# A linear-attention layer and a gated unit: q in token order, permuted transposes, new loads, stores and work order

## The chip, the cores and the metric

The kernel runs on one core of a Trainium2 chip. Its engines each follow their own instruction queue: PE (TensorE, matmuls), ACT (ScalarE, exponentials and evictions), DVE (VectorE), POOL (GpSimd, which also issues DMAs) and SP (SyncE, which here only issues DMAs). Engines wait for each other by semaphores. The time of a kernel is the device time of one execution in microseconds (us).

## The reference

Eight batches, eight heads, 576 tokens, head size 64, 128 random features; the model width is 512. Inputs and output are float32.

```
def phi(x):
    proj = einsum('bhsd,df->bhsf', x, w_phi)
    proj = proj - max(abs(proj), axis=-1, keepdims=True)
    return concatenate([exp(proj), exp(-proj)], axis=-1)
q_p, k_p = phi(q), phi(k)
kv  = einsum('bhsf,bhsd->bhfd', k_p, v)
z   = sum(k_p, axis=2)
num = einsum('bhsf,bhfd->bhsd', q_p, kv)
den = einsum('bhsf,bhf->bhs', q_p, z)[..., None] + 1e-06
x   = (num / den), heads side by side                # (8, 576, 512)
gate = sigmoid(causal convolution of x over 5 tokens, per channel)
out  = (gate * (x @ w_val)) @ w_out                  # (8, 576, 512)
```

## The kernel before

**Attention of one batch.** k and q of a batch are 4608 rows of 64 numbers each. They lie in SBUF with 128 rows by 36 columns of 64, two columns side by side make 18 blocks of 128 by 128, and the blocks are transposed so that PE can contract over the head size. Five units (four of 4 blocks, one of 2) go through PSUM. For k: `kp` projects a unit (L577), `kmax` (L585, DVE) takes the largest absolute value of each row, `kexp` (L595, ACT) makes exp(proj) and exp(-proj), two instructions of 1024 elements for a full unit. The maxima are not subtracted from k's projections; `ek` (L604, ACT) makes a factor of them, and `vs` (L610, POOL) multiplies v by it, four times per batch. `st` (L620, PE) contracts features with scaled v and a column of the factor, which gives kv and z together, and `kv` evicts it. For q: `qm` projects (L577), `qmax` takes maxima (L585), `mqt` and `mqr` transpose and negate them, `rx` (L682, POOL) spreads them over a block pattern, `qp` (L693 and L698, PE) computes features by tokens and adds the negated maxima with a second matmul, and `qexp` (L706, ACT) makes the two exponentials. Its last, half unit is written with four instructions into a tile of its own, `QTT` (L709). `num` (L719, L726) multiplies by kv and z, and `nrm` (L737, L740, DVE) divides.

**Order of q's tokens.** q is read as one flat array, 36 consecutive rows to a partition, so a unit holds tokens from all over the sequence. Every `num` task of a batch therefore waits for all ten exponentials of q (`allq`), and its output rows are tokens in steps: x comes out in two halves of 144 columns, and tokens 16 and 17 of each run of 18 land in a fifth, half-size piece.

**The gated unit of one batch.** Normalised x is transposed, 128 by 128, by PE (`xtp`, L748, L752) and copied (`xtc`); for batches 6 and 7 (`XB`) two of the three parts go by DMA transposes instead (`xtd`, L755). `halo` (L768, L769, POOL) copies the columns that the convolution needs from the other half. `gate` (L781) is 80 matmuls of 64 by 64 with diagonal weights, `tanh` (L785, ACT) makes the sigmoid, `val` (L791) 32 matmuls, `gv` (L797, DVE) the product, `gvc` (L805, POOL) collects the tokens of the fifth piece of two batches, `out` (L813; L817 for that piece) the output matmuls, `oev` evicts, `odma` (L830, L836) stores rows of 2 KB.

**Loads.** Batch 0's k and q come as float32 from SP's queue and are transposed as float32 (`tp32`, L536). Later batches come as bf16 from POOL's queue, one DMA for k and one for q (L550), batch 1 transposed on PE (L555), batches 2 to 7 by DMA transposes from SP's queue (L565). v comes from SP's queue, batch 1's from POOL's. A copy of one column (`hold`, L509, L512) on POOL keeps a load behind the transpose that frees its buffer.

**The order of the work.** `build` lists tasks with what they wait for. `ORDER` is the list in which they are written out: each engine runs its own tasks in that order, whatever is ready. `FLEX` says which engine takes a task that several could take, `BANKS` which PSUM banks a group of tasks uses. `WARM` and `ZERO` insert dummy matmuls at places of the order; those of `ZERO` add zeros to a finished result (L497, L504).

Of the kernel before, what the change touches and what calls it, by code (L numbers as in the profile page):

```python
# [24 lines left out]
NU = len(UNITS)  # L25
PEB = 1
QPART = ((0, 1), (2, 3, 4))
XB = (6, 7)
HOLDU = 4
NO = 8  # L30
NJ = 2 * NC
XH = R // 2
HALO = 16
XW = HALO + XH
# [4 lines left out]
STD = 1.18  # L39
E1 = D + 1  # L40
QW = 2 * NR

ORDER = (
# [36 lines left out]
)  # L80
FLEX = (
    "AAAAAADAAADDPPPPDDDDAADDDDDDDDDDDDDAAADAAAADDDDAAADDDAADAAADDADAADDDDADDDDADDDDDDAADADDAAAAAA"
)
BANKS = (
    "037362307001454523232323016701676714232367230101676012354423010145454501013660564675601456745010145450101676767014501454"
    "545672012376701230167676745677773567232367232345452301672323232367674545015452343623670101232345454452230145450167676767"
    "010123014501230167450120167364012345236745454555723014545234567232323010123236745230167232346701422010167454567010121656"
    "701456701012301670123010167232367674567023677260123230123230167464644501016701670123676745672345232345450123670157672345"
    "010167452326322345670145670101674545012345012367452345010127452301014545670101765"
)  # L90

# [809 lines left out]
```

## Time and profile before

| what | us |
|---|---|
| runs | 216.2, 217.88, 246.94 (median 217.88) |
| span of the profiled execution, first to last instruction | 215.4 |
| PE busy | 194.6 (90%) |
| ACT busy | 180.6 (84%) |
| DVE busy | 170.2 (79%) |
| POOL busy | 132.9 (62%) |

The profile shows one execution. Its device time outside of the profile is not known; its span is 0.8 us under the fastest of the runs. A row of a group names a line, an engine, an operation, the tile written and the tiles read, a count, the busy time and the mean time of one. A row of the timeline or of the chain begins with its start and its length in us. Matmuls overlap each other: 72 state matmuls of 191 ns each take 1.16 us together, so a chain row divided by its count is the price of one in a row of many.

### The profile page before, as it was taken

To read this page: it belongs to the slowest core of one execution; us is meant where nothing else is said; L and a number is where in the kernel's file an instruction comes from. 1 tells how busy PE (TensorE), PEld (TensorE's weight loads), DVE (VectorE), ACT (ScalarE), POOL (GpSimd) and SP (SyncE) were. 2 spreads that over 40 slices of the span, in tenths; PEclk is the share of its full clock that TensorE was granted. 3 is DMA by queue.
4 is the path that set the end of the run, shared out by engine and by line. 5 is a ranking of instruction groups with operands and counts; after the bars stand their busy time and mean duration, and the time that the engine had idled before them with its cause. 6 is when DMAs were issued, how large, how long until landed. Compare 5 with 4: busy or idle time off the path is not lost.

```text
span 215.4 us, 9005 instructions
## 1 busy us (share of the span) xinstructions
PE 194.6 (90%) x3924; PEld 138.9 (64%) x3944; DVE 170.2 (79%) x257; ACT 180.6 (84%) x267; POOL 132.9 (62%) x172
## 2 busy tenths in 40 slices
PE   2887978778999999989999999999999999899990
PEld 2665566566766767667767677568757766687640
DVE  3299999999699978998899978998699897654510
ACT  3699999999999899998899997999988988634251
POOL 3045999996984649952997099903992879210010
PEclk9999999999999999999999999999999999999998
DMA  6999979999799699979997878979962264864166
GB/s 180 381 226 208 291 162 159 277 198 199 139 165 286 118 153 250 290 130 200 237 279 134 96 165 251 188 151 173 287 211 84 67 161 126 83 168 99 49 188 205
DMA packets 49954, 39.92 MB, mean 185 GB/s; under 512 B 34165, under 2 KB 39541, under 8 KB 49914
## 3 DMA queue, kind: packets, MB, share of 16 engines
q1 hardware_dynamic: 43616, 28.65, 56.8%
q0 software_dynamic: 6032, 10.49, 26.2%
q8 instruction: 31, 0.51, 1.0%
q10 hardware_dynamic: 266, 0.21, 0.3%
q14 instruction: 9, 0.07, 0.1%
HBM read 30.48 MB, written 9.44 MB: 185 GB/s over the span
## 4 chain that ended last, share of the span: by engine, by line
PE 55%; ACT 18%; DVE 15%; issue 4%; DMA 4%; SPq 0%; DVEq 0%; ACTq 0%
PE PS L791 12%; PE PS L781 9%; PE PS L813 9%; ACT QTIL L706 7%; ACT KTIL L595 7%; DVE MQP L585 6%; PE PS L719 5%; PE PS L577 5%; PE PS L620 4%; DVE MK L585 2%; PE PS L693 2%; DMA KTIL<-in_k_dram 2%; DMA XT<-XN 2%; PE PS L536 2%; DVE XN L740 2%
## 5 line engine op out<-in xcount | busy, mean ns | idle before, releaser
L595 ACT ACTIVATE KTIL<-PS 128x1024 bf16<-128x1024 f32 (+1 forms) x80 | 71.8, 965 | 3.5 <-PE PS L577 1.7
L610 POOL TENSOR_TENSOR VT<-VN,EK 128x1152 bf16<-128x1152 f32 x32 | 67.9, 2123 | 2.9 <-ACT EK L604 2.8
L706 ACT ACTIVATE QTIL<-PS 128x1024 bf16<-128x1024 f32 x64 | 62.5, 1051 | 1.9 <-PE PS L698 1.4
L682 POOL TENSOR_TENSOR RX<-MQR,ident 128x512 bf16<-128x512 bf16 (+1 forms) x39 | 36.6, 963 | 36.2 <-DVE MQR L670 32.8
L585 DVE TENSOR_REDUCE MK<-PS 128x8 f32<-128x1024 f32 (+1 forms) x40 | 44.3, 1113 | 2.9 <-PE PS L577 1.2
L585 DVE TENSOR_REDUCE MQP<-PS 128x8 bf16<-128x1024 f32 (+1 forms) x40 | 43.6, 1112 | 2.1 <-PE PS L577 1.2
L791 PE MATMUL PS<-XT,WV 128*128 128x288 bf16 x256 | 34.8, 286 | 0.3 <-DVE GV L797 0.2
L797 DVE SCALAR_TENSOR_TENSOR GV<-TH,PS 128x576 bf16<-128x576 bf16 x32 | 23.8, 752 | 10.4 <-PE PS L791 4.7
L813 PE MATMUL PS<-WOUT,GV 128*128 128x512 bf16 x110 | 29.7, 380 | 1.1 <-issue 0.2
L791 PEld LDWEIGHTS <-WV 128*128 128x128 bf16 x256 | 23.8, 98 | 7.9 <-issue 1.4
L785 ACT ACTIVATE TH<-PS 128x576 bf16<-128x576 f32 x32 | 20.4, 663 | 9.3 <-PE PS L781 5.9
L781 PE MATMUL PS<-XT,GW 64*64 64x288 bf16 x640 | 23.2, 285 | 0.8 <-DMA XT<-XN 0.7
L620 PE MATMUL PS<-VT,KTIL 64*128 64x65 bf16 x1152 | 23.1, 191 | 0.7 <-issue 0.6
L740 DVE TENSOR_TENSOR XN<-PS,RCP 128x512 bf16<-128x512 f32 x32 | 22.1, 692 | 1.4 <-DMA XT<-XN 0.3
L620 PEld LDWEIGHTS <-KTIL 64*128 64x128 bf16 x1152 | 20.7, 95 | 3.3 <-issue 2.3
L719 PEld LDWEIGHTS <-QTIL 128*128 128x128 bf16 x512 | 18.3, 97 | 6.4 <-issue 4.1
L719 PE MATMUL PS<-KV,QTIL 128*128 128x65 bf16 x512 | 20.3, 193 | 0.4 <-DVE MQP L585 0.2
L781 PEld LDWEIGHTS <-GW 64*64 64x64 bf16 x640 | 17.8, 106 | 3.4 <-issue 0.8
L634 ACT ACTIVATE OUTS<-PS 128x512 f32<-128x512 f32 x22 | 13.5, 619 | 7.3 <-PE PS L813 6.1
L813 PEld LDWEIGHTS <-GV 128*128 128x128 bf16 x128 | 11.1, 98 | 11.3 <-issue 0.6
L577 PE MATMUL PS<-W,qT 64*128 64x128 bf16 x288 | 15.2, 219 | 2.7 <-ACT QTIL L706 1.0
L577 PEld LDWEIGHTS <-qT 64*128 64x128 bf16 x288 | 10.7, 95 | 9.1 <-issue 4.3
(79 smaller groups left out, 235.0 us busy)
## 6 DMA issues: line engine op xcount, KB each, us to landing
out_dram<-OUTS SPq DMA_DIRECT2D x32, 256.0 KB, 3.4
VN<-in_v_dram SPq DMA_DIRECT2D x7, 1152.0 KB, 6.4
KQN<-in_q_dram POOLq DMA_DIRECT2D x6, 576.0 KB, 8.3
KQN<-in_k_dram POOLq DMA_DIRECT2D x6, 576.0 KB, 9.6
KTIL<-in_k_dram SPq DMA_DIRECT2D x4, 288.0 KB, 4.3
VN<-in_v_dram POOLq DMA_DIRECT2D x1, 1152.0 KB, 11.5
KTIL<-in_q_dram SPq DMA_DIRECT2D x4, 256.0 KB, 5.0
out_dram<-OUTS SPq DMA_DIRECT2D x14, 64.0 KB, 2.4
```

The source lines that it names most:

```text
L577: nc.tensor.matmul(self.PS[:, t.grp.banks[par], i * P:(i + 1) * P], X[rows, (c0 + i) * P:(c0 + i + 1) * P], self.W2[rows, :], start=True, ...
L585: self.nc.vector.tensor_reduce(o, self.two(t.grp, n * P).rearrange("p a (c f) -> p a c f", f=F), AX.X, ALU.max, apply_absolute_value=True)
L595: self.nc.scalar.activation(self.KTIL[b % 2][:, s, c0:c0 + n, :, :].rearrange("p c a f -> p a c f"), self.two(t.grp, n * P).rearrange("p a ...
L610: nc.gpsimd.tensor_tensor(self.VT[g][:, s, :, 0:D], self.VN[b % 2][:, NC * g:NC * g + NC, :], e.to_broadcast([P, NC, D]), ALU.mult)
L620: nc.tensor.matmul(self.PS[:, t.grp.banks[ab], (s * 2 + x) * E1:(s * 2 + x + 1) * E1], self.KTIL[b % 2][rows, s, J // 2, J % 2, :], self.V ...
L682: self.nc.gpsimd.tensor_tensor(o, *wide(self.MQR[self.mq(b, u)][:, :], self.ident2), ALU.mult)
L706: self.nc.scalar.activation(o, i, AF.Exp, scale=1.0 - 2.0 * s)
L719: nc.tensor.matmul(self.PS[:, t.grp.banks[h // 4], (h % 4) * E1:(h % 4 + 1) * E1], Q[:, s, c % 2, h, (c // 2) * P:(c // 2 + 1) * P], self. ...
L740: nc.vector.tensor_tensor(o.rearrange("p (g h) d -> p g h d", g=ng), n[:, :, :, 0:D], rc.unsqueeze(3).to_broadcast([P, ng, 4, D]), ALU.mult)
L781: self.nc.tensor.matmul(self.PS[o * D:(o + 1) * D, t.grp.banks[par], 0:R], self.GW[r, jj, 4 - m, :], X[r, 4 * a + jj, :, HALO - 8 * s:HALO ...
L791: self.nc.tensor.matmul(self.PS[:, t.grp.banks[par], 0:R], self.WV[:, i, (2 * j + par) * D:(2 * j + par + 2) * D], X[:, 4 * par + i, :, HA ...
L813: nc.tensor.matmul(self.PS[:, t.grp.banks[0], :], GV[:, j, c % 2, (c // 2) * XH:(c // 2) * XH + P], self.WOUT[:, j, c % 2, :], start=(j == ...
```

## The change

The kernel is written anew around another order of q's tokens; the arithmetic is the same.

- q is loaded as bf16 in five pieces of 128 tokens (the last of 64) for all heads, each token run of 8 rows to a partition. A unit then holds consecutive tokens, `num(b, c)` waits only for the two exponentials of unit c and for kv, and `QTIL` holds all tokens in sequence. `QTT`, `GVT`, `halo`, `gvc`, `hold` and the 144-column halves are gone.
- The transposes of x multiply by a permuted identity (`perm`) instead of the identity, which puts the tokens of a transposed block in order. All go through PE; `xtd` is gone.
- Gate, tanh, value and product of batches 0 and 7 are done in two column parts, 0 to 128 and 128 to 288 (`COLS`).
- All of k, q and v, batch 0 too, come from POOL's queue; batch 0 is cast to bf16 by its load and transposed as bf16. SP keeps the DMA transposes and the stores.
- A store writes two consecutive tokens per partition, 4 KB rows; the last one goes in two. The tails of two batches (64 tokens each) share one eviction and two stores.
- `ORDER`, `FLEX` and `BANKS` are new, banks come in pairs (0,1), (2,3), (4,5), (6,7), `ZERO` is gone and `WARM` has two entries. The reciprocal is a task of its own.

```diff
+KLOAD = (((0, 1), (1, 1), (2, 2)), ((0, 4),))
+QLOAD = ((tuple((i, 1) for i in range(5)),) * 2)
+NO = 4
+COLS = {b: ((0, R),) for b in range(B)}
+COLS[0] = ((0, P), (P, R))
+COLS[B - 1] = ((0, P), (P, R))
-    "60:6:1 81:1:1 87:7:2 134:7:1 141:7:1 "
-ZERO = "35:76:7 61:80:5 75:34:1 101:105:1 126:215:8 144:223:1 155:192:4 158:200:1 175:315:6 189:346:1 195:241:2 197:241:2 211:327:1"
+    "11:7:5 54:5:1 "
...
+            for i, (p0, n) in enumerate(KLOAD[b > 0] if w == "k" else QLOAD[b > 0]):
+                x = A("l" + w, b, i, "POOL", fn("load", w, b, p0, n), [G("xd" + w, b - 1)])
...
+                x = A("xp", b, 0, "SP", fn("xpose", w, b), sorted(set(land[w]), key=lambda t: t.idx) + war)
...
+            x = A("lv", b, 0, "POOL", fn("loadv", b), [G("vs", b - 2, g, s) for g in range(2) for s in range(2)])
...
-        allq = [G("qexp", b, u, s) for u in range(NU) for s in range(2)] + [G("kv", b, i) for i in range(2)]
...
-            num = h["num", b, c] = A("num", b, c, "PE", 0.57 if c < 4 else 0.38, fn("num", b, c), allq,
-                                     g, 0 if c < 4 else 2)
+            num = h["num", b, c] = A("num" if c < 4 else "num4", b, c, "PE", fn("num", b, c),
+                                     [h["qexp", b, c, s] for s in range(2)] + [h["kv", b, i] for i in range(2)], g, 0 if c < 4 else 2)
...
-                if i < 2 and b in XB:
-                    xt = h["xtp", b, i] = A("xtp", b, i, "SP", 1.4, fn("xtd", b, i), nrms + war, lat=-0.2)
...
+        for z, (x0, x1) in enumerate(COLS[b]):
+            xs = [h["xtc", b, i] for i in range(3) if i * P < x1 and min(R, (i + 1) * P) > x0 - (1 if x0 else 0)]
+            for j in range(4):
+                g = plan.group("gate", 2)
+                gt = h["gate", b, j, z] = A("gate", b, j, "PE", fn("gate", b, j, x0, x1), xs + h["gw"], g, 3, n=x1 - x0)
...
-        self.QTIL = TT("QTIL", 2, [P, 2, 2, H, 2 * P])
+        self.QTIL = TT("QTIL", 2, [P, 2, H, S])
...
+        for i, n in enumerate((4, 2)):
+            nc.vector.tensor_copy(self.perm[i][:, :].rearrange("p (z x y) -> p z y x", x=8, y=n),
+                                  ident_f[:, :].rearrange("p (z y x) -> p z y x", x=8, y=n))
...
+    def load(self, t, w, b, p0, n):
+        N = self.N[w][b]
+        if w == "k":
+            o = N[:, :, :].rearrange("p y c -> p (y c)").rearrange("p (hp x) -> p hp x", hp=4)[:, p0:p0 + n, :]
+            self.nc.gpsimd.dma_start(o, self.rows("k", b)[:, p0:p0 + n, :])
+            return
+        x = self.src["q"][b]
+        c0 = 4 * p0
+        if p0 < 4:
+            self.nc.gpsimd.dma_start(N[:, c0:c0 + 4, :].rearrange("p y c -> p (y c)"), x[:, p0 * P:(p0 + 1) * P, :].rearrange("h (i t) d -> h i (t d)", i=16))
+        else:
+            self.nc.gpsimd.dma_start(N[:, 16:18, :].rearrange("p y c -> p (y c)"), x[:, 4 * P:S, :].rearrange("h (i t) d -> h i (t d)", i=16))
...
-        if u < 4:
-            o = self.QTIL[b % 2][:, s, :, :, :].rearrange("p a h (k r) -> p a (h k) r", k=2)[:, :, :, u * 32:(u + 1) * 32]
-            self.nc.scalar.activation(o, i, AF.Exp, scale=1.0 - 2.0 * s)
-        else:
-            for a in range(2):
-                self.nc.scalar.activation(self.QTT[:, s, :, a, :].rearrange("p h (k r) -> p h k r", k=2),
-                                          i[:, a, :, :].rearrange("p (h k) r -> p h k r", k=2), AF.Exp, scale=1.0 - 2.0 * s)
+        o = self.QTIL[b % 2][:, s, :, u * P:u * P + n * 32].rearrange("p h (a r) -> p a h r", a=2)
+        self.nc.scalar.activation(o, self.two(t.grp, n * P).rearrange("p a (h r) -> p a h r", h=H), AF.Exp, scale=1.0 - 2.0 * s)
...
-            for y in range(8):
-                nc.tensor.transpose(ps[:, y * P:(y + 1) * P], self.XN[i][:, y // 4, (y % 4) * P:(y % 4 + 1) * P], self.ident[:, :])
+            o = ps.rearrange("p (a j u r) -> p u j a r", a=2, j=4, u=2)
+            for u in range(2):
+                for j in range(4):
+                    nc.tensor.transpose(o[:, u, j], self.XN[i][:, u, j * P:(j + 1) * P], self.perm[0][:, :])
...
+    def out4(self, t, b):
+        for j in range(4):
             for a in range(2):
+                for i in range(2):
                     p0 = a * D + i * 32
+                    self.nc.tensor.matmul(self.PS[p0:p0 + 32, t.grp.banks[0], :], self.GV[(b - 1 + i) % 3][:, j, a, 2 * P:R],
+                                          self.WOUT[:, j, a, :], start=(j == 0), stop=(j == 3))
...
+    def store(self, t, b, kk):
+        d = self.out_d[b][2 * P * kk:2 * P * (kk + 1), :].rearrange("(r a) o -> r (a o)", a=2)
+        self.nc.sync.dma_start(d, self.OUTS[(2 * b + kk) % NO][:, :, :].rearrange("p a o -> p (a o)"))
...
+    def store4(self, t, b, a):
+        eng = self.nc.scalar if t.eng == "ACT" else self.nc.sync
+        d = self.out_d[b - 1:b + 1, 4 * P:S, :].rearrange("i (r a) o -> a i r o", a=2)[a]
+        eng.dma_start(d, self.OUT4[b // 2 % 2][a * D:(a + 1) * D, :])
```

More of the change, by code (lines that the diff above doesn't have):

```diff
@@ L90 @@
 )
 class Task:
-    __slots__ = ("kind", "b", "u", "engs", "durs", "fn", "deps", "grp", "also", "opens", "mode", "eng", "lat", "idx", "wait", "rank")
+    __slots__ = ("kind", "b", "u", "engs", "fn", "deps", "grp", "opens", "mode", "eng", "idx", "n")
 class Group:
     __slots__ = ("kind", "nb", "left", "banks", "idx")
-def out_seq(b, c):
-    return 9 * (b // 2) + (4 * (b % 2) + c)
-LAT = {"PE": 0.17, "ACT": 0.17, "DVE": 0.17, "POOL": 0.2, "SP": 0.7, "DMA": 1.3}
-MSW = 0.05
-def dve(n, ov=0.075):
-    return n / 960.0 + ov
@@ L147, in follow @@
     def follow(self):
-        names = {"A": "ACT", "D": "DVE", "P": "POOL"}
+        names = {"A": "ACT", "D": "DVE", "P": "POOL", "S": "SP"}
         for t, f in zip([t for t in self.tasks if len(t.engs) > 1], FLEX):
@@ L160, in parts, with pieces @@
     return QPART if b == 0 else (tuple(range(NU)),)
+def pieces(b):
+    return ((0, 8), (8, 8), (16, 2)) if b else ((0, 4), (4, 4), (8, 8), (16, 2))
+VE = ("DVE", "ACT")
 def build(plan, em=None):
@@ new lines, in build @@
+            h["idf"] = A("idf", 0, 0, "POOL", fn("c_idf"))
+            h["id"] = A("idb", 0, 0, "DVE", fn("c_idb"), [h["idf"]])
+            h["idc"] = A("idc", 0, 0, "DVE", fn("c_idc"), [h["idf"]])
+            x = A("lw", b, 0, "SP", fn("c_w"))
+            x = A("DMA", b, 0, "DMA", None, [x], n="lw")
+            h["w"] = A("wc", b, 0, "DVE", fn("c_w2"), [x])
+            x = A("lcw", b, 0, "SP", fn("c_cv"))
+            h["lcw"] = A("DMA", b, 0, "DMA", None, [x], n="lcw")
+        land = {"k": [], "q": []}
@@ L256, in build @@
[L256 to L259 removed]
+        if True:
+            x = A("lv", b, 0, "POOL", fn("loadv", b), [G("vs", b - 2, g, s) for g in range(2) for s in range(2)])
+            h["lv", b] = A("DMA", b, 0, "DMA", None, [x], n="lv")
@@ new lines, in build @@
+        if b == 0:
+            x = A("wv", b, 0, "POOL", fn("c_wv"), [])
+            x = A("DMA", b, 0, "DMA", None, [x], n="wv")
+            h["wv"] = A("wvx", b, 0, "POOL", fn("c_wvx"), [x])
+            x = A("wo", b, 0, "POOL", fn("c_wo"), [])
+            h["wo"] = x = A("DMA", b, 0, "DMA", None, [x], n="wv")
+            x = A("wod", b, 0, "SP", fn("c_dupo"), [x])
+            h["wod"] = A("DMA", b, 0, "DMA", None, [x], n="wod")
+            g = plan.group("cw", 1)
+            x = A("cw", b, 0, "PE", fn("c_cw"), [h["lcw"], h["idf"]], g, 0)
+            x = A("cw2", b, 0, "DVE", fn("c_cw2"), [x], g)
+            h["gw"] = [A("cgt", b, i, "POOL", fn("c_gt", i), [x, h["idc"]]) for i in range(2)]
@@ L330, in build @@
-                g = plan.group("xtp", 1)
-                xt = h["xtp", b, i] = A("xtp", b, i, "PE", 0.54 if i < 2 else 0.22, fn("xtp", b, i), nrms, g, 0)
-                h["xtc", b, i] = A("xtc", b, i, ("DVE", "ACT"), (dve(512), act(1024)) if i < 2 else (dve(256), act(256)), fn("xtc", b, i), [xt] + war, g)
-        halo = A("xtc", b, 3, "POOL", 0.6, fn("halo", b), [G("xtc", b, 2)] + [G("gate", b - 2, j) for j in range(4)])
-        xall = [G("xtc", b, i) for i in range(3)] + [halo]
-        for j in range(4):
-            g = plan.group("gate", 2)
-            gt = h["gate", b, j] = A("gate", b, j, "PE", 0.62, fn("gate", b, j), xall, g, 3)
-            h["tanh", b, j] = A("tanh", b, j, "ACT", act(576), fn("tanh", b, j), [gt, G("gv", b - 1, j)], g)
@@ new lines, in gvs @@
+        def gvs(b, x0, x1):
+            return [h["gv", b, j, z] for j in range(4) for z, (y0, y1) in enumerate(COLS[b]) if y0 < x1 and y1 > x0]
+        for kk in range(2):
+            oes = []
+            war = stores[-NO] if len(stores) >= NO else None
+            for a in range(2):
+                g = plan.group("out", 1)
+                o = h["out", b, 2 * kk + a] = A("out", b, a, "PE", fn("out", b, a, kk), gvs(b, kk * P, kk * P + P) + [h["wod" if a else "wo"]], g, 0)
+                oes.append(A("oev", b, a, VE, fn("oev", b, a, 2 * b + kk), [o, war], g))
+                if b == B - 1 and kk == 1:
+                    x = A("st1", b, a, ("SP", "ACT"), fn("store1", b, kk, a), [oes[a]])
+                    x = A("DMA", b, a, "DMA", None, [x], n="st1")
+            if not (b == B - 1 and kk == 1):
+                x = A("st2", b, kk, "SP", fn("store", b, kk), oes)
+                x = A("DMA", b, kk, "DMA", None, [x], n="st2")
+                stores.append(x)
@@ new lines, in build @@
+        if b % 2:
+            g = plan.group("out4", 1)
+            o = A("out4", b, 4, "PE", fn("out4", b), gvs(b, 2 * P, R) + gvs(b - 1, 2 * P, R) + [h["wod"]], g, 4)
+            h["out", b, 4] = h["out", b - 1, 4] = o
+            oe = A("oev", b, 4, VE, fn("oev4", b), [o, G("st4", b // 2 - 2, 0), G("st4", b // 2 - 2, 1)], g)
+            for a in range(2):
+                x = A("st4", b, a, ("SP", "ACT") if b == B - 1 else "SP", fn("store4", b, a), [oe])
+                h["st4", b // 2, a] = A("DMA", b, a, "DMA", None, [x], n="st4")
@@ L365 @@
+    return plan
+EKS = (0,)
+VSD = (0,)
 class Emit:
@@ L859 @@
             warm[int(i)] = (int(bank), int(n))
-        zero = {}
-        for x in ZERO.split():
-            i, k, n = x.split(":")
-            zero[int(i)] = (int(k), int(n))
         for i, t in enumerate(plan.follow()):
-            for _ in range(zero[i][1] if i in zero else 0):
-                em.zero(plan.tasks[zero[i][0]])
             for _ in range(warm[i][1] if i in warm else 0):
```

488 lines of the change are left out of this document (158 added, 330 removed), and 75 rows, old and new, of the table ORDER.

## The prediction

> **What bounds the kernel now.** I read the page's first two parts, then the stretches, then the chain of waits in order of time, and last the groups. The page's shares alone mislead: three engines are over 79% busy, each the limit somewhere else.
>
> ```profile
> span 215.4 us, 9005 instructions
> PE 194.6 (90%) x3924; PEld 138.9 (64%) x3944; DVE 170.2 (79%) x257; ACT 180.6 (84%) x267; POOL 132.9 (62%) x172
> ```
>
> The stretches (start and end, length, then busy time of PE, PEld, DVE, ACT and POOL, granted clock, DMA share, GB/s) separate them:
>
> ```profile
> 5.00:10.00 5.00, 4.29 (x31) 3.36 (x31) 0.45 (x2) 3.08 (x5) 0.00 (x0) 1.00 1.02 370
> 30.00:40.00 10.00, 7.31 (x261) 5.98 (x259) 9.54 (x13) 9.94 (x14) 10.00 (x11) 1.00 1.00 220
> 160.00:170.00 10.00, 9.95 (x232) 7.10 (x232) 8.58 (x11) 9.04 (x15) 5.20 (x6) 1.00 0.22 57
> 200.00:210.00 10.00, 9.95 (x61) 5.60 (x62) 3.69 (x5) 4.16 (x8) 1.05 (x4) 1.00 0.44 128
> ```
>
> At 30 to 40 us ACT is full (9.94 of 10) and PE is not: the attention of the first batches feeds PE too little. At 160 us PE is full and ACT waits now and then. At 200 us PE alone is full: the two last gated units are run off while ACT and DVE are half idle. The timeline and the chain date the turns and give the price of each PE task:
>
> ```profile
> 51.11 1.56 PE L781 MATMUL PS<-XT,GW 64*64 64x288 bf16 x40
> 184.75 1.25 ACT L709 ACTIVATE QTT<-PS 128x256 bf16<-128x256 f32 x4
> ```
> ```profile
> 94.12 0.89 PE PS L748 x16
> 125.28 0.37 PE PS L726 x16
> 133.63 1.16 PE PS L620 x72
> 149.34 0.98 PE PS L719 x32
> 162.27 0.55 PE PS L577 x16
> 180.65 0.21 PE PS L693 x2
> 180.86 0.22 PE PS L698 x2
> 183.74 4.44 DMA XT<-XN
> 195.35 3.19 PE PS L781 x100
> 199.51 3.92 PE PS L791 x32
> 203.43 3.24 PE PS L813 x15
> 209.47 1.00 PE PS L817 x8
> 210.54 0.60 ACT OUTS L634
> ```
>
> The first gate runs at 51.1 us, the last exponential of attention ends at 186.0, PE ends at 210.5, and eviction and store of the last tile take the other 4.9 to 215.4. Per batch these rows give PE: gate 80 at 31.9 ns = 2.55 us; value 32 at 122.5 = 3.92; output 16 at 216 = 3.46 and half a pair of tails 0.50; state 144 at 16.1 = 2.32; numerator 64 at 30.6 = 1.96 and tail 0.37; projections 72 at 34.4 = 2.48; q features 4.5 units at 0.43 = 1.94; transposes of x 18 at 55.6 = 1.00. Sum **20.5 us**, 164.0 for eight batches, 162.2 with the 32 transposes that DMA does here. By the written order, before the first gate PE has done 208 projections (7.15), 8.5 units of q features (3.66), 216 state matmuls (3.48), one numerator (2.33) and one set of transposes (1.0): 17.6. So 144.6 us of PE work take the 159.4 us from 51.1 to 210.5: **a density of 0.907**, in which the 4.44 us wait for the DMA transpose of x lies. From 51 us on the time is PE's work over that density; before it, it is the time to the first gate.
>
> **The change part by part.**
>
> *q in sequence.* Before, each numerator task waits for all ten q exponentials, because a unit holds scattered tokens; after, unit c holds tokens 128c to 128c+127 and its numerator waits for two. With the first batch's gated unit split at column 128, the first gate needs only two normalised units. By the changed order, PE has before it: projections of k and q for two batches (144, 4.95), one batch of q features (1.94), state (2.32), numerator (2.33), transposes (1.0): 12.5 instead of 17.6, and 72 bf16 transposes of the inputs.
>
> When is that? The queue of loads decides. The order issues k0, k1, all of q0, four pieces of q1, two of q2, then v0: 6.2 MB of float32 at the 370 GB/s of the 5 to 10 us row is 16.6 us, and 3 us to a first landing, so v0 is there at about 20.
>
> ```profile
> 8.68 1.94 ACT L595 ACTIVATE KTIL<-PS 128x1024 bf16<-128x1024 f32 x2 [0.39 <-PE PS L577]
> 58.34 2.12 POOL L610 TENSOR_TENSOR VT<-VN,EK 128x1152 bf16<-128x1152 f32 x1
> 60.55 2.12 POOL L610 TENSOR_TENSOR VT<-VN,EK 128x1152 bf16<-128x1152 f32 x1
> 78.10 4.61 POOL L682 TENSOR_TENSOR RX<-MQR,ident 128x512 bf16<-128x512 bf16 x5 [4.39 <-DVE MQR L670]
> 66.11 3.77 ACT L595 ACTIVATE KTIL<-PS 128x1024 bf16<-128x1024 f32 x4
> ```
>
> POOL then does two scalings of v (2.21 each, start to start), three q maxima (2.6 of the 4.61) and one more scaling (the fourth is DVE's): 29 us. State, eviction, numerator, normalising, transposes and copy add 4 to 5. ACT arrives there too: its first exponential is at 8.7 us now, behind float32 transposes, and comes at about 7.5 by my estimate; it has 24 by then, 20 of them at 0.94 and four at half, five copies and two evictions, some 25 us, so 32.5. The first gate comes at **34 us** (31 if loads overlap better, 40 if they land late), 17 us earlier than now.
>
> *PE's total.* 164.0 - 12.5 = 151.5 us are left after the first gate; 151.5 / 0.907 = 167.0. With 34 before and 4.9 behind: **205.9 us of span**. The 6.9 us more of PE work behind the first gate are in it, 1.8 of them the transposes that come back from DMA; the 4.44 us wait leaves with them but is not taken off again, since it is part of the density. What is late next is ACT.
>
> *ACT and DVE.*
>
> ```profile
> L709 ACT ACTIVATE QTT<-PS 128x256 bf16<-128x256 f32 x32 | 10.0, 420 | 1.5 <-PE PS L698 1.3
> L595 ACT ACTIVATE KTIL<-PS 128x512 bf16<-128x512 f32 x16 | 8.8, 602 | 1.5 <-PE PS L577 1.3
> L634 ACT ACTIVATE OUTS<-PS 128x512 f32<-128x512 f32 x22 | 13.5, 619 | 7.3 <-PE PS L813 6.1
> L628 DVE COPY XT<-PS 128x1024 bf16<-128x1024 bf16 x10 | 6.7, 683 | 0.0
> ```
>
> 16 exponentials of 512 (9.6) replace 32 of 256 (10.0); three evictions fewer (-1.9), four KV copies of the same size more (+2.5), eight tanh parts more (about +1). ACT's 180.6 stay. DVE gets four copies of x (+2.7), three evictions (+2.1), one scaling of v and the split parts, loses four KV copies: some +6 on 170.2. Both fit in 206 us, but then ACT is busy 88% of it and DVE 85%, more than now, and PE's work with the front is 168; three engines so evenly loaded wait for each other. That is why I don't raise the density above today's, though the 4.44 us wait is gone.
>
> *The end.* After the last q exponential the changed order leaves three numerators (1.5), four outputs (3.46), transposes (1.0), gate, value, output and tail of the last batch (2.55, 3.92, 3.46, 1.0): 16.9 us; now it is 210.5 - 186.0 = 24.5. The column parts add 16 tasks with the same columns in all; at 65 columns a matmul already runs at 16.1 ns, so parts of 128 and 160 cost between nothing and 1 us, and I take 0.
>
> *Loads on POOL.* Five pieces of q and one v per batch go through POOL.
>
> ```profile
> L550 POOL DMA_DIRECT2D KQN<-in_q_dram x6 | 3.5, 589 | 0.5 <-issue 0.5
> L531 POOL DMA_DIRECT2D VN<-in_v_dram x1 | 0.8, 813 | 0.0
> L805 POOL COPY GVT<-GV 128x128 bf16<-128x128 bf16 x16 | 4.4, 323 | 11.0 <-DVE GV L797 11.0
> L768 POOL COPY XT<-XT 128x224 bf16<-128x224 bf16 x8 | 3.0, 374 | 12.9 <-DVE XT L628 6.7 <-ACT XT L632 6.2
> ```
>
> Each load also waits until the load eight before it has landed, and the first q piece until the last batch's q is transposed; behind it in POOL's order stand VT, for which the state matmuls wait, and RX, for which the q features wait.
>
> 33 issues of q at 0.589 (+19.4), seven of v at 0.81 (+5.7), three of k (+2.3); gone are the tail copies (-4.4), halo copies (-3.0 and about -2 for their second half), holds, one scaling (-2.1): 132.9 becomes about 148. Hidden as long as POOL reaches its last q maximum before about 175 us; without that cover it is the second rival. A quarter-size piece could cost POOL as little as half an issue (-10 us) or a whole k issue of 0.78 (+6); neither moves the end while it is hidden.
>
> *Fill and stores.*
>
> ```profile
> L504 PE MATMUL PS<-ONES,NIL 64*128 64x128 bf16 x140 | 5.6, 216 | 0.0
> ```
>
> These zero matmuls go (eight wider ones too); most lie in PE's idle time before 51 us. The 36 float32 transposes of the first batch become bf16 at 55.6 ns (2.0 us): also front time. 4 KB store rows halve the store issues on SP; nothing waits for them but the last, and only reuse of four output tiles. The last store is 256 KB instead of the tail's 64 KB, 3.4 against 2.6 us to landing: +0.8, within the 4.9. Bank pairs change no duration that I can see: 0.
>
> **Against a rule, DMA.** The Trainium skill, "DMA: Bandwidth & Descriptors", section on why a DMA increments its semaphore by 16 ("How many engines (k)"), says that a transfer is spread over the largest number of engines up to 16 that divides both access patterns' slowest dimension. By it q pieces (8 heads outermost) use 8 engines and the tail stores (2 batches outermost) use 2. No run here shows it yet; by its figure of 27 GiB/s per engine my estimate for a 128 KB tail store on two engines is 2.3 us of data instead of 0.3, and the sum would be 2 us longer at most.
>
> **The rivals.**
>
> *Load chain, slower.* There is one q buffer. So per batch: q transposed, five issues in POOL's order, landing, wait in SP's queue (where stores now stand between transposes), transpose.
>
> ```profile
> KQN<-in_q_dram POOLq DMA_DIRECT2D x6, 576.0 KB, 8.3
> qT<-KQN SPq DMA_TRANSPOSE x6, 5.5
> DMA to landing us min/median/max: 7.0/9.0/14.7
> ```
>
> In POOL's changed order the five issues of batches 3 to 7 are spread over 6, 9, 15, 4 and 7 us of its work: 8.2 + 8.3 + 5.5 = 22.0 per batch, against 167 / 7.4 = 22.6 per batch that PE takes. At the maximum of 14.7 it is 28.4. It decides from 23; at 26 the last five batches cost 3.4 each: 206 + 17 = 223, and at 28.4 it is 235. For it: no slack, in-order waits. Against: the last piece is a quarter of the size and need not take 8.3.
>
> *ACT sets the pace, no change.* Of ACT's 180.6 busy us about 25 lie before 32.5 us and 8.6 behind the last exponential (the last batch's tanh and five evictions). The 147 between take 148 at the share of the 30 to 40 us row (0.994) and 163 at that of the 160 us row (0.904), where it waits for PE. The latter puts the last exponential at 195, and 195 + 16.9 + 4.9 = 217: PE's head start is then spent waiting for ACT, and the change doesn't do what it is for. For it: nothing is taken off ACT. Against: at 0.904 ACT waits for a PE that is full, and PE is ahead here.
>
> *Clock.* Early matmuls run at half speed although the clock column says 1.00:
>
> ```profile
> 8.56 1.57 PEld L536 LDWEIGHTS PS<-ident_f,KTIL 128*128 128x128 f32 x8 [0.20 <-issue]
> 15.11 0.64 PEld L536 LDWEIGHTS PS<-ident_f,KTIL 128*128 128x128 f32 x6
> ```
>
> 196 ns each at 8.6 us, 107 at 15.1. Without the zero matmuls the half speed may last until the first gate: 12.5 + 4.0 of work would take 33 of the 34 us, the first gate moves to about 40, span 212. That this gate needs sustained activity of about 3.4 us and falls back after an idle window of that length is the rule of the Trainium skill, "TensorE: Matmul & The Clock Gate", part 1; the two rows agree with the two speeds, the window is shown by no run here.
>
> **How the numbers follow.** Span against runs: 215.4 lies 0.8 under the fastest run and 2.5 under the median of 217.9. I add 1.6: 205.9 + 1.6 = **207.5 us**. Chances: forecast 0.58 (own range 197 to 212; the low end is density 0.97, 34 + 156 + 4.9 + 1.6), clock or late loads at 213.5 0.12, ACT's pace at 218 0.13, load chain at 223 or more 0.17. 2%, about what a measurement of this kernel can tell from no change, is 213.5 to 222.2: faster 0.66 (the forecast and two thirds of the clock case), same 0.17, slower 0.17. The range is 197 to 224.
>
> **What would show it.** First gate near 34 us; PE over 9.5 in each 10 us from 45 on; DVE and ACT over 9; 17 us between the last q exponential and PE's end; no DMA wait for x. Wrong if PE or ACT wait for qT or POOL's VT or RX by several us per batch, if POOL waits at its loads, or if PE's matmuls before 30 us have twice their length.

## The result, and the profile after

The changed kernel takes 246.12 us (median of 245.32 to 246.24), the kernel before 217.8 beside it: a ratio of 1.131, 95% interval 1.126 to 1.137. It is **13% slower**. The forecast was 207.5, with a range to 224. Each time below is the median of a kernel's fast runs, those within 1.5% of its fastest; four profiles are of a slower run (tail stores 242.9 us, the clock 252.2, "later" 240.4, "k first" 231.1), so what they show is read by place and not by the length of the whole.

The page of the changed kernel: span, busy time, and the granted clock in 40 slices of the span.

```profile
span 244.5 us, 9212 instructions
...
PE 198.9 (81%) x4068; PEld 143.8 (59%) x4082; DVE 174.9 (72%) x275; ACT 178.5 (73%) x259; POOL 150.7 (62%) x171
...
PEclk9999776959999999859999999968999999999995
```

The work is what was forecast: ACT 178.5 (180.6 were to stay), DVE 174.9 (176), POOL 150.7 (148), PE 4 us more than before. What is new is waiting, and it lies in certain stretches (columns as in the prediction's fence):

```profile
100.00:110.00 10.00, 4.21 (x38) 2.39 (x38) 2.28 (x3) 3.56 (x6) 3.60 (x6) 0.66 0.82 212
...
180.00:190.00 10.00, 9.95 (x231) 7.42 (x230) 9.18 (x12) 9.90 (x15) 8.62 (x9) 1.00 0.61 170
```

At 180 us it runs as hoped. At 100 us all five engines stand idle most of the time, while the DMA engines are 82% busy. The chain of waits (start, length, what) names what they wait for; the last two rows are the end of the kernel:

```profile
37.63 13.47 DMA qT<-KQN
...
67.21 10.09 DMA qT<-KQN
...
90.80 15.03 DMA qT<-KQN
...
128.25 5.54 DMA qT<-KQN
...
154.95 6.20 DMA qT<-KQN
...
231.71 2.60 PE PS L714 x12
...
234.34 0.60 ACT OUTS L489
```

Five times the chain runs through a transpose of q, 50.3 us together. The waits (engine and line, for whom, total, times, longest) show both ends of it, PE behind the transpose and POOL's next q load behind the same transpose:

```profile
POOL KQN L475 <- DMA qT<-KQN: 21.1, 4, 9.6
PEld L513 <- DMA qT<-KQN: 19.0, 5, 6.3
PE PS L513 <- DMA qT<-KQN: 17.3, 5, 5.8
```

Where the 38.6 us between the forecast's span (205.9) and this one lie: the first gate comes at 44.8 and not at 34 (+10.8); from it to PE's end, at 234.3, are 189.5 us and not 167.0 (+22.5); from there to the last store 10.2 and not 4.9 (+5.3). In the second part PE stands idle 18.8 us in seven gaps over 0.7 us.

The transposes of q, in the view of one tile. Before:

```profile
L565 SPq DMA_TRANSPOSE qT<-KQN x6: 3182/3424/3573, 31.1 to 144.9; - x6
...
DMA to landing us min/median/max: 5.0/5.5/6.4
```

After:

```profile
L500 SPq DMA_TRANSPOSE qT<-KQN x6: 2619/3910/8569, 37.6 to 180.9; - x6
...
DMA to landing us min/median/max: 4.6/9.8/15.0
```

The first row's last two times are the starts of the first and the last of six. A fifth of their difference is the **distance** from one batch's q to the next: 22.8 us before, 28.7 after. I use it below for every kernel.

The trace's packets show what goes with a long transpose. A transpose moves 2304 packets of 256 bytes. From its issue to its last packet, all 12 transposes of the kernel before took 4.1 to 5.6 us, and at most 0.1 MB from POOL's queue moved meanwhile. In the changed kernel the seven with less than 0.1 MB beside them took 4.1 to 5.3; the other five 12.8, 11.6, 10.0, 7.3 and 7.1, with 2.2, 0.9, 1.2, 1.2 and 0.4 MB of k, q, v and weights beside them. (The third of these five waited 5.2 of its 10.0 us behind the transpose before it in the same queue.) The Trainium skill, "DMA: Bandwidth & Descriptors", section "Queues, rings and completion order", says that a DMA engine takes packets in turn from the queues that have work for it. The trace agrees in direction: it is the transposes that stretch. A 256-byte packet takes 18 ns in the median, the loads' packets of 1,024 to 4,608 bytes 98 to 178 ns; if these are what is taken in turn, a packet of a transpose waits out a much longer one. That this turn is the cause is argued here and not shown.

### The profile page after: what moved, and what is told of

Read it like the earlier page. It is cut to its first block, busy times and chain, and to the rows that moved or that the text cites. A ratio compares the mean times of both kernels' runs of the same rounds, so it can differ in the third digit from the quotient of the medians.

```text
span 244.5 us, 9212 instructions
## 1 busy us (share of the span) xinstructions
PE 198.9 (81%) x4068; PEld 143.8 (59%) x4082; DVE 174.9 (72%) x275; ACT 178.5 (73%) x259; POOL 150.7 (62%) x171
## 4 chain that ended last, share of the span: by engine, by line
PE 48%; DMA 24%; ACT 8%; POOL 7%; issue 5%; DVE 4%; DVEq 0%; POOLq 0%; ACTq 0%
DMA qT<-KQN 21%; PE PS L702 9%; PE PS L714 8%; PE PS L692 7%; PE PS L557 6%; PE PS L513 5%; PE PS L639 4%; DMA KTIL<-in_q_dram 4%; ACT QTIL L629 3%; POOL VT L547 3%; PE PS L618 2%; DVE MQP L521 2%; ACT KTIL L531 2%; PE PS L623 2%; PE PS L670 2%
## 5 line engine op out<-in xcount | busy, mean ns | idle before, releaser
L629 ACT ACTIVATE QTIL<-PS 128x1024 bf16<-128x1024 f32 (+1 forms) x80 | 70.0, 963 | 10.4 <-PE PS L623 9.5
L702 PE MATMUL PS<-XT,WV 128*128 128x288 bf16 (+2 forms) x320 | 35.8, 263 | 1.6 <-ACT TH L696 0.7
L513 PE MATMUL PS<-W,qT 64*128 64x128 bf16 x288 | 16.9, 240 | 20.0 <-DMA qT<-KQN 17.3
L714 PE MATMUL PS<-WOUT,GV 128*128 128x512 bf16 x115 | 31.4, 386 | 0.8 <-issue 0.2
L696 ACT ACTIVATE TH<-PS 128x576 bf16<-128x576 f32 (+2 forms) x40 | 21.0, 568 | 14.5 <-PE PS L692 14.4
L702 PEld LDWEIGHTS <-WV 128*128 128x128 bf16 x320 | 26.1, 98 | 8.8 <-issue 3.4
L708 DVE SCALAR_TENSOR_TENSOR GV<-TH,PS 128x576 bf16<-128x576 bf16 (+2 forms) x40 | 24.7, 630 | 6.3 <-PE PS L702 5.2
L475 POOL DMA_DIRECT2D KQN<-in_q_dram x24 | 15.1, 632 | 21.7 <-DMA qT<-KQN 21.1
L692 PE MATMUL PS<-XT,GW 64*64 64x288 bf16 (+2 forms) x800 | 25.2, 274 | 0.0
L639 PE MATMUL PS<-KV,QTIL 128*128 128x65 bf16 x512 | 20.5, 198 | 0.6 <-DVE XN L660 0.4
L489 ACT ACTIVATE OUTS<-PS 128x512 f32<-128x512 f32 x16 | 9.4, 613 | 12.9 <-PE PS L714 12.9
```

Of the source, the lines that this page charges most:

```text
L513: nc.tensor.matmul(self.PS[:, t.grp.banks[par], i * P:(i + 1) * P], X[rows, (c0 + i) * P:(c0 + i + 1) * P], self.W2[rows, :], start=True, ...
L629: self.nc.scalar.activation(o, self.two(t.grp, n * P).rearrange("p a (h r) -> p a h r", h=H), AF.Exp, scale=1.0 - 2.0 * s)
L639: nc.tensor.matmul(self.PS[:, t.grp.banks[h // 4], (h % 4) * E1:(h % 4 + 1) * E1], Q[:, s, h, c * P:(c + 1) * P], self.kvh(b, s, h), start ...
L692: self.nc.tensor.matmul(self.PS[o * D:(o + 1) * D, t.grp.banks[par], 0:x1 - x0], self.GW[r, jj, 4 - m, :], X[r, 4 * a + jj, HALO - s + x0: ...
L702: self.nc.tensor.matmul(self.PS[:, t.grp.banks[par], 0:x1 - x0], self.WV[:, i, (2 * j + par) * D:(2 * j + par + 2) * D], X[:, 4 * par + i, ...
L708: nc.vector.scalar_tensor_tensor(out=self.GV[b % 3][:, j, :, x0:x1], in0=self.TH[j][:, :, x0:x1], scalar=1.0, in1=self.two(t.grp, x1 - x0) ...
```

## The experiments

Theory **collision**: loads on POOL's queue run into the transposes on SP's, and these get longer. Theory **one buffer** (the prediction's load chain): whatever a transpose takes, the next q is asked for only when the last is transposed, in five issues between POOL's other work. Three further runs (245.0, 244.4, 234.8 us) computed something else and are not used for the account: in the first, with two q buffers, output tiles were overwritten before their store; in two early arrangements of the loads k of batch 4, in one of them also of batch 5, was loaded over k of the batch before it was transposed. The second run still says one thing. It was expected at 216 to 224 us, or 228 to 238, and took 244.4 although its six transposes of q took only 4.1 to 5.3 us to their last packet: short transposes of q alone are not enough.

**v behind the transposes.**

```diff
-x = A("lv", b, 0, "POOL", ...)
+x = A("lv", b, 0, "SP" if b else "POOL", ...)   # and in ORDER behind the transposes
```

> The changed kernel, but v of batches 1 to 7 is loaded from SP's queue, behind the transposes of k and q that it met on the way (batch 1's behind q's transpose of batch 2, and so on). Nothing else is moved. Theory 'collision': SP's DMA transposes take 7 to 13 us from issue to their last packet where loads from POOL's queue are in flight, and 4 to 5 where none are; with v out of the way the two longest (12.8 us for batch 2, 11.6 for batch 4) fall to 5 to 8, and the time from 246 to 226 to 236. Theory 'one buffer': what sets the pace is that q of a batch is asked for only when the last batch's q is transposed, in five issues spread over POOL's work; the transposes get shorter but the next q pieces are late all the same, and the time stays between 240 and 248.

241.5 us, 4.6 less.

```profile
L501 SPq DMA_TRANSPOSE qT<-KQN x6: 2613/3050/7802, 37.4 to 172.6; - x6
```

The time lies in the range of "one buffer". The transposes follow the collision theory in part: that of q of batch 4 went from 11.6 to 6.1 us, that of batch 2 still met the output weights and k (9.3 us), and that of k of batch 3 went from 5.2 to 14.3, with v of batch 1 now ahead of it in SP's own queue. The distance is 27.0. v is only a part of what collides, and moved to SP's queue it can be in the way there.

**q loads together.**

```diff
-  214 215 225 230 240      # places of the five loads of batch 3 in ORDER; 4 to 7 alike
+  214 215 216 217 218
```

> The changed kernel, but the five q loads of each batch from 3 on stand one behind the other in POOL's order, at the place of the first. Before, they were spread over 5.7, 9.1, 14.9, 3.6 and 15.0 us in the trace. Theory 'one buffer': the last piece lands 5 to 12 us earlier in batches 4, 5 and 7, and the time falls to 226 to 236. Theory 'collision': the transposes still meet v and k, and the time stays between 242 and 249.

237.7 us, 8.4 less, between the two ranges and nearer to "one buffer". In the changed kernel POOL spreads one batch's q over 9 us:

```profile
77.86 0.68 POOL L475 DMA_DIRECT2D KQN<-in_q_dram  x1 [1.48 <-DMA qT<-KQN]
...
82.98 0.67 POOL L475 DMA_DIRECT2D KQN<-in_q_dram  x1
...
86.31 1.24 POOL L475 DMA_DIRECT2D KQN<-in_q_dram  x2
```

Between them stand two scalings of v and two spreads of maxima. Here collisions stayed (14.0 us for batch 2), so both theories hold a part.

**Tail stores by rows.**

```diff
-d = self.out_d[b - 1:b + 1, 4 * P:S, :].rearrange("i (r a) o -> a i r o", a=2)[a]
-eng.dma_start(d, self.OUT4[b // 2 % 2][a * D:(a + 1) * D, :])
+for i in range(2):
+    d = self.out_d[b - 1 + i, 4 * P:S, :].rearrange("(r a) o -> a r o", a=2)[a]
+    eng.dma_start(d, self.OUT4[b // 2 % 2][a * D + i * 32:a * D + i * 32 + 32, :])
```

> The changed kernel, but each store of the tails (64 partitions, two batches of 32 rows as its slowest dimension) is issued as two stores of 32 rows. In the trace the two last tail stores ran with at most two packets at a time and ended 8.6 us behind PE's end. If the number of engines of a store follows from its slowest dimension, the last store lands with the others, about 5 us behind PE's end: 246 to 240 to 242. If the end is slow for another reason, such as the 4 KB rows or the issues on SP, nothing changes or it gets 0.5 us worse by two issues more: 245 to 247.

236.0 us, 10.1 less and more than expected; ratio to before 1.088 (1.082 to 1.094). Its profile (span 241.1 us) ends 4.6 us behind PE's last matmul (236.6), where the changed kernel needs 10.2. That is 5.6 of the 10.1, about what was expected; where the other 4.5 come from is not shown. In the changed kernel the 64 packets of ACT's tail store ran from 236.5 to 242.9 us, never more than two at a time, while the other tail store and the last full store were under way too; with 32 rows as the slowest dimension the same 64 packets took 0.9 us, up to 16 at a time. The Trainium skill, "DMA: Bandwidth & Descriptors", section on why a DMA increments its semaphore by 16, which the prediction weighed, gives two engines for such a store, and the trace agrees. It adds that a store from SP or ACT takes the lowest-numbered ones; both tail stores would then share the same two, which the trace, without engine numbers, does not show.

**One part in the kernel before: v from POOL.**

```diff
-ld = A("lv", b, 0, "POOL" if b == 1 else "SP", ...)
+ld = A("lv", b, 0, "POOL" if b in (1, 3, 4, 5, 6, 7) else "SP", ...)   # behind the last scaling of b - 2
```

> The kernel before with one part of the change alone: v of batches 3 to 7 is loaded from POOL's queue as soon as its buffer is free (behind the last scaling of v of the batch before last) and no longer from SP's queue behind the transposes. Theory 'collision': these loads now meet the transposes of k and q of the same batch, which go from 4.1 to 5.6 us (issue to last packet) to 7 to 12, and the time from 217.5 to 221 to 235. Theory 'one buffer', or no collision: v is only earlier, 216 to 219.

226.8 us against 217.2: a ratio of 1.044, interval 1.032 to 1.056. The chain of this run:

```profile
97.81 0.64 POOL VN L532
98.45 13.15 DMA kT<-KQN
```

and the transposes of k, which now come first behind that load:

```profile
DMA to landing us min/median/max: 6.4/9.2/13.1
```

To their last packet k's transposes of batches 3 to 7 took 6.7 to 11.9 us, in the kernel before 4.2 to 5.6. Five loads of v moved into their way cost 9.6 us in a kernel without any of the other parts. With them POOL also got their five issues (137.2 us busy instead of 132.9); the chain runs through the transposes, as the row of 13.15 us shows.

**The three edits together.**

> The three edits that each helped alone, together and with nothing else: v behind the transposes on SP's queue (4.6 us alone), q loads together (8.4), tail stores by 32 rows (about 6 to 10). If they act at separate places, 246 - 23 = 223, range 220 to 227. If they shorten the same waits, 228 to 236.

235.3 us, in the range of "the same waits". The profiles say more. From PE's last matmul to the end it is 4.6 us instead of 10.2, the gain of the tail stores. But that matmul ends at 229.4 us, with q together alone at 225.5 and with v behind alone at 228.5: ahead of the end, the two together gain less than each of them alone. The output weights, batch 1's v and k of batch 3 still met transposes (15.2 us for batch 3's k), and the distance is 26.8.

**All loads into the gaps.**

```diff
-wo 162, lv1 165 POOL, xp2k 173, lk3 186, xp2q 192, lq3 214..240, lv2 310, lv3 336, lk4 345, ...
+wo 93, xp2k 172, lv1 173 SP, xp2q 191, lq3 213..217, lk3 218, lv2 219, xp3k, xp3q, lv3 SP, lq4 + lk4, ...
```

> The changed kernel with its loads and transposes in the pattern of the kernel before: the five q loads of a batch and its k load stand together in POOL's order, the transposes of k and q of a batch follow, v comes behind them from SP's queue (batch 2's from POOL's, batch 1's behind the first transpose); the output weights are loaded earlier; tail stores in pieces of 32 rows. If collisions, spread and tail stores are what was added, 216 to 228, the transposes at 4 to 6 us. If one q buffer sets the pace whatever the transposes take, the distance from one q transpose to the next stays at 26 us or more and the time is 230 to 240.

226.4 us, ratio to before 1.042 (1.036 to 1.048): 19.7 of the 28.3 us are gone (span of its profile 224.1).

```profile
L501 SPq DMA_TRANSPOSE qT<-KQN x6: 2662/3022/4359, 36.5 to 160.8; - x6
...
DMA to landing us min/median/max: 5.2/5.5/7.2
```

All twelve transposes take 4.1 to 5.8 us to their last packet, and PE has no gap over 1.8 us behind the first 6. The distance is 24.9, still 2.1 over the kernel before.

**The clock.**

```diff
-    "11:7:5 54:5:1 "
+    "11:7:5 54:5:1 155:4:10 224:6:22 369:6:7 495:4:26 648:2:7 776:4:15 "
```

> The changed kernel with 87 dummy matmuls of 512 columns ahead of the six tasks at which PE waited longest in its trace (10 ahead of a state task at 33 us, 22, 7, 26, 7 and 15 ahead of q projections of batches 2 to 6), into the bank that the task then overwrites. The waits stay as long; only the clock behind them can differ. In the trace, projections behind waits of 2.3 us and more took 0.61 to 0.65 us for eight instead of 0.40, for 4 to 7 us each. If that half speed is on the path it is worth 4 to 9 us: 246 to 237 to 242. If the load chain sets the time anyway and PE's slow stretches hide in it, 244 to 248.

247.1 us, no gain, and in part the edit missed its aim: at 35 us the dummy matmuls waited for the same bank as the task.

```profile
35.38 0.41 PE L455 MATMUL PS<-ONES 128*128 128x512 bf16 x1 [2.40 <-DVE MQP L521]
36.01 3.37 PE L455 MATMUL PS<-ONES 128*128 128x512 bf16 x8 [0.22 <-issue]
39.31 1.33 PE L557 MATMUL PS<-VT,KTIL 64*128 64x65 bf16 x72
```

Behind them the state took 1.33 us instead of 2.16, but began 4.3 us later. What can be read: the granted clock's mean rose from 0.926 to 0.966 and the distance stayed, 28.3 (40.9 to 182.5). Half speed is there; by this one run the chain of loads does not depend on it.

**Is it an engine?** From the arranged kernel, work was taken off POOL, ACT and PE in turn.

```diff
 def vs(self, t, b, g, s):
+    if b and g and s: return          # POOL
 def kexp(self, t, b, u, s):
+    if b > 1 and u < 2 and s: return  # ACT
 def val ... def out ...
+    3 of 4 partial sums where b > 1   # PE
```

> The arranged kernel of 226.4 us, with one of the four scalings of v in batches 1 to 7 left out (the second feature sign of heads 4 to 7, so the state of those batches is made from an older scaled v). It takes 7 times 2.3 = 16 us from POOL, about as much as the change's load issues put on it. If POOL's work is hidden, as the prediction says, nothing changes: 225 to 228. If POOL is on the path where the chain shows it, 226 to 215 to 222.

> The arranged kernel of 226.4 us, with two of k's ten exponentials left out in each of the batches 2 to 7 (the second sign of units 0 and 1, so the state there is made from older features): 12 times 0.905 = 10.9 us less on ACT. If ACT sets the pace up to the last q exponential (201.5 us), 215 to 219. If PE does, 223 to 227. If the two wait for each other in turn, about half: 219 to 223.

> The arranged kernel of 226.4 us, with a quarter of the value matmuls (8 of 32) and of the output matmuls (4 of 16) left out in batches 2 to 7, so the sums there lack one part: 6 times 1.84 = 11 us less on PE, of which about 2.7 lie behind the last q exponential and are gained in any case. If PE sets the pace, 214 to 218. If ACT does, 222 to 225.

226.4, 225.4 and 224.3 us: none gains more than the 2.7 us of PE work behind the last q exponential. By busy time POOL did 15.5 us less, ACT 9.5 and PE 6.8. That exponential ended at 201.7, 201.0 and 202.2 us, in the arranged kernel at 201.5. The transposes of q, in the order POOL, ACT, PE:

```profile
L501 SPq DMA_TRANSPOSE qT<-KQN x6: 2662/2740/4227, 36.7 to 162.3; - x6
```
```profile
L501 SPq DMA_TRANSPOSE qT<-KQN x6: 2682/2712/3611, 37.7 to 161.0; - x6
```
```profile
L501 SPq DMA_TRANSPOSE qT<-KQN x6: 2662/2708/4287, 37.6 to 162.2; - x6
```

The distances are 25.1, 24.7 and 24.9. None of these three engines sets the pace alone by its amount of work. A rival is left: the limits may lie so close together that another takes over. In the arranged kernel the chain runs through POOL and DMA from 122 to 162 us; with less on POOL it runs from 57 to 146 us through PE, ACT and short issues alone, and the distance stays:

```profile
96.87 1.97 PE PS L695 x55
...
111.68 1.84 ACT QTIL L632 x2
```

Two engines at once were not relieved, and DVE (174.6 us busy) not at all.

**Load groups later, earlier, k first.**

```diff
-lq3 213, lq4 383, lq5 489, lq6 628, lq7 781      # places of the groups in ORDER
+lq3 247, lq4 391, lq5 518                        # later
+lq4, lq5 behind xp3q, xp4q; lq6, lq7 amid the scalings of batches 4, 5   # earlier
+lk ahead of the five lq of its group             # k first
```

> The arranged kernel of 226.4 us, with the load groups of batches 3, 4 and 5 moved a few tasks back in POOL's order, behind the scalings of v that stood behind them. In its chain, POOL's scalings of v and load issues of 43 to 60 us and 69 to 77 us are the work that ended last. If POOL's 4.4 us of issues per group delay the state matmuls behind them, 226 to 221 to 225. If what counts is when q lands, the transposes come later and it is 226 to 231.

236.5 us, outside both ranges: three groups were moved back, all five came 7 to 14 us later, and that costs 10. PE now waits for k, 10.7 us where it waited 3.2:

```profile
PEld L514 <- DMA kT<-KQN: 10.7, 4, 4.0
```

> The arranged kernel of 226.4 us, with the load groups of batches 4 to 7 moved forward in POOL's order, to where POOL stands when the last batch's q has been transposed. In the trace of the arranged kernel these groups are issued 3.3, 2.2, 6.1 and 5.1 us behind the end of that transpose. Moving groups back cost 11 us. If the chain of loads and transposes sets the pace, moving them forward gives 4 to 10 us back: 216 to 222. If after the arrangement PE, ACT or POOL's scalings set it, 225 to 231.

230.2 us, 3.8 more, distance 25.9: the second range, and no gain from issuing earlier. The transposes took no longer (5.4 us median to landing). The state matmuls waited longer for the scalings of v, which now stood behind the groups. In the arranged kernel, and in this one:

```profile
PE PS L558 <- POOL VT L549: 3.3, 3, 1.7
```
```profile
PE PS L558 <- POOL VT L549: 6.3, 4, 4.0
```

> The arranged kernel of 226.4 us, with k's load ahead of the five q loads in each group of batches 3 to 7 instead of behind them. With 11 us less work on ACT, 11 less on PE or 16 less on POOL the last q exponential ended at 201.0 to 202.2 us as before, and q's transposes came every 24.7 to 24.9 us: the chain of loads and transposes is left. In it k's transpose comes first and waits for k, which lands last. If that chain sets the pace, k lands 3 to 5 us earlier, its transpose runs while q lands, and five batches give 6 to 15 us back: 211 to 220. If only the last landing of the group counts, or the transposes now meet the q loads, 223 to 230.

226.9 us: no gain. k landed 6 to 10 us behind its group's first issue instead of 11 to 13, but its transpose met the q loads (5.4 to 9.1 us to the last packet instead of 4.1 to 5.3).

```profile
L501 SPq DMA_TRANSPOSE kT<-KQN x6: 3462/4023/6189, 31.0 to 159.6; - x6
...
DMA to landing us min/median/max: 5.5/7.4/8.9
```

The arranged kernel's own chain from 120 to 160 us goes twice through the same round:

```profile
122.34 1.18 POOL KQN L476 x2
...
124.61 7.84 DMA KQN<-in_k_dram
132.47 4.57 DMA kT<-KQN
...
138.57 2.08 POOL VT L548
...
147.41 1.69 POOL KQN L476 x3
149.10 8.62 DMA KQN<-in_k_dram
157.74 4.74 DMA kT<-KQN
```

Issues, landing, transpose, scalings of v, next issues. It is not the whole answer: the run with less on POOL takes one scaling out of each round, and its distance is 25.1. What sets the 24.9 is therefore not shown. Each order that I tried traded one wait for another, and none beats the kernel before; whether another order would is open, and a second q buffer was not tried in a form that computes the same.

## Why the prediction was wrong

**The step that failed** is the one that made PE's density the pace: "151.5 / 0.907 = 167.0". It took 189.5, since PE was not the bound: it stood idle 18.8 us in seven gaps, and the granted clock was half for about 7 us around or behind three of them. The rival that it called "Load chain" came true, with 0.17 where it needed most of the chance; that a single q buffer is what it takes is not shown. Its own sum, 8.2 + 8.3 + 5.5 = 22.0 against 22.6, had no slack, and the 5.5 was taken from a trace in which at most 0.1 MB from POOL's queue moved beside a transpose. With loads beside them the transposes of q took 9.8 in the median and 15.0 at most to landing; the issues were spread over 9.7 us in the mean instead of 8.2 (batch 7's over 15.0, not 7); the distance became 28.7. The rival priced 28.4 at 235 us; with the late first gate and the tail on top that is 251, 5 us over the measured 246. The stated range ended at 224, short of what the rival's own price allowed. The prediction asked of each load what POOL pays for the issue, and never which transfer it meets.

**The first gate**, 34 forecast, 44.8 measured. POOL's part was to end at 29 and ended at 34:

```profile
23.18 2.12 POOL L547 TENSOR_TENSOR VT<-VN,EK 128x1152 bf16<-128x1152 f32 x1 [0.84 <-DMA VN<-in_v_dram]
...
30.52 3.24 POOL L547 TENSOR_TENSOR VT<-VN,EK 128x1152 bf16<-128x1152 f32 x1
```

v landed at 23 instead of 20, and the third scaling took 3.24 us instead of 2.12. The state then waited 1.2 us more for a maximum on DVE. From its start the 4 to 5 us for state, numerators, normalising and transposes were 9.9, with PE at half speed for the first 6 of them:

```profile
17.02 0.61 PE L513 MATMUL PS<-W,qT 64*128 64x128 bf16 x8
...
23.55 0.28 PE L494 MATMUL PS<-ident,QTIL 128*128 128x128 bf16 x2 [1.20 <-DMA QTIL<-in_q_dram]
...
25.75 0.66 PE L513 MATMUL PS<-W,qT 64*128 64x128 bf16 x8
...
30.32 0.40 PE L513 MATMUL PS<-W,qT 64*128 64x128 bf16 x8
...
34.97 2.16 PE L557 MATMUL PS<-VT,KTIL 64*128 64x65 bf16 x72 [2.26 <-DVE MQP L521]
...
44.84 0.85 PE L692 MATMUL PS<-XT,GW 64*64 64x128 bf16 x40
```

So the **clock** rival named a real thing, for most of the way to the first gate and beyond it. Matmuls ran at half speed up to 20.5 us (the kernel before had the full speed by 12.9, as its row below shows), from 23.9 to 27.3 and from 34.1 to 40.9, and after the first gate for 3 to 6 us behind each wait of 3.4 us and more. How much of the first gate's 10.8 us this makes is not shown: the run with dummy matmuls reached only the wait at 33 us, and changed the work there.

```profile
12.85 0.39 PE L577 MATMUL PS<-W,qT 64*128 64x128 bf16 x8
```

**ACT and DVE**: their work was forecast within about 2 us. ACT's pace alone, as a rival, is refuted for the arranged kernel: 9.5 us less on ACT moved the last q exponential by 0.5 us. In the changed kernel ACT waits for PE.

**The end**: 16.9 us behind the last q exponential were forecast. Its row ends at 215.9, PE at 234.3, so 18.4; the column parts cost little. The last store was forecast at +0.8, "within the 4.9"; the stretch behind PE's end is longer by 5.3. The Trainium skill's rule against the change was weighed and priced at up to 2 us, from one store alone; two such stores and the last full one were under way together.

```profile
212.15 3.77 ACT L629 ACTIVATE QTIL<-PS 128x1024 bf16<-128x1024 f32 x4
```

**POOL**: the sum was right (148 and 150.7) and so was "hidden", as amount: 15.5 us less on POOL gained nothing in the arranged kernel. Where in its order the issues stand does count: 8.4 us for the spread alone, and 10 for a shift of three groups.

**Of the signs** named beforehand, "PE wait for qT by several us per batch" and "POOL waits at its loads" both came, and so did "PE's matmuls before 30 us have twice their length" (eight projections 0.61 to 0.66 us at 6 to 17 and at 24 to 27 us, 0.40 at full speed); PE over 9.5 without a break came only from 170 us on.

**The account**: 19.7 of the 28.3 us are the places and queues of the loads, the places of the transposes and the tail stores, shown by one arrangement that changes nothing else (6.0 us of it behind PE's end). The other 8.6 are located and not explained: in the spans, a distance of 24.9 instead of 22.8 (10.5 us over five batches) and a later first transpose (36.5 against 31.1), less some 7 us that are saved behind the last transpose. The gain that the change was forecast to bring, gates 17 us earlier, was 6.3 us here and 8.2 in the arranged kernel, and is given back before the last q exponential.

## What to carry to other kernels

Before a load is moved to another queue, look up which transfers it will then meet; a duration of a DMA transpose holds only for the traffic that it was measured in. Where a buffer is single, write down the round of issue, landing, transpose and next issue, and compare it with the work per round. When they are as close as 22.0 and 22.6 here, do not count on either to hide the other; here, taking 7 to 16 us of work off one engine then gained 2 us at most. Look at a store's slowest dimension: 32 instead of 2 made the end 5.6 us shorter.

## What the runs showed of the hardware

- A DMA transpose of 590 KB took 4.1 to 5.6 us to its last packet with at most 0.1 MB of POOL's loads beside it, and up to 14.0 beside 2.3 MB of them (the run with q together); a load of v put ahead of the transposes of five batches cost 9.6 us in the kernel before.
- 64 packets of 2 KB of a store took 6.4 us, never more than two at a time, with a slowest dimension of 2, and 0.9 us, up to 16 at a time, with one of 32.
- PE fell to half speed behind 2.26 us of idle time (72 state matmuls in 2.16 us, 1.33 at full speed), but also behind 1.20 (at 23.6 us, above) and, in the arranged kernel, behind 1.73 (second row: 54 of them in 1.67 us), and not behind 1.70 (first row). The length of the last wait alone does not decide:

```profile
77.35 0.29 PE L513 MATMUL PS<-W,qT 64*128 64x128 bf16 x4 [1.70 <-DMA qT<-KQN]
```
```profile
77.31 1.67 PE L558 MATMUL PS<-VT,KTIL 64*128 64x65 bf16 x54 [1.73 <-POOL VT L549]
```
